# Sinkhorn attention into a gated MLP on one core: the V round trip in halves, another order of the units, the bias off TensorE

## The chip, the cores and the metric

One core of one Trainium2 chip runs the kernel. Its engines are TensorE (PE, with PEld for weight loads), VectorE (DVE), ScalarE (ACT), GpSimd (POOL) and SyncE (SP); each works through its own queue in order, and the two queues of SP and POOL issue all DMAs here. The metric is device time in us. The kernel before took 233.57 us, the median of 3 runs (233.11 to 235.1).

## What is computed

Batch 4, 8 heads, 768 tokens, head size 64, 8 blocks of 96 tokens. A Sinkhorn iteration turns a small matrix per head into mixing weights P; k and v are mixed over blocks with P, q attends within its block, and the result goes through a gated MLP.

```python
for _ in range(5):
    P = P - np.max(P, axis=-1, keepdims=True)
    P = np.exp(P)
    P = P / (np.sum(P, axis=-1, keepdims=True) + 1e-09)
    P = P / (np.sum(P, axis=-2, keepdims=True) + 1e-09)
k_sorted = np.einsum('bhij,bhjcd->bhicd', P, k_b)      # v_sorted likewise
scores = scale * np.matmul(q_b, k_sb.transpose(0, 1, 2, 4, 3))
attn = softmax(scores)                                 # within a block
x = np.matmul(attn, v_sb)                              # -> (B, S, H * D) = (4, 768, 512)
h = np.maximum(x @ w_in, 0.0)                          # d_ff 1024
u, v = h[..., :512], h[..., 512:]
v_n = (v - mu) / np.sqrt(var + 1e-06)
v_s = np.einsum('ts,bsd->btd', w_spatial, v_n) + b_spatial[None, :, None]
out = (u * v_s) @ w_out
```

## The kernel before

Tokens are laid out six to a partition (128 x 6 = 768). Attention of one batch is a list of units. `vmix` (line 234) multiplies v by `pdiag`, a block form of P, for two heads at a time; ACT copies the result into `vm`. After the fourth, the whole `vm` (780 KB) goes to DRAM (`vd`, line 247), and six DMAs bring it back as `vb` (line 250) with the 96 tokens of a block on the partitions. `qtr` and `ktr` bring q and mixed k to head-size-major form; `score` (line 294) and ACT's exponential give `ex`; `attend` (line 316) multiplies `ex` by `vb`, whose 65th column of ones yields the row sums; DVE divides (lines 323, 324). `xtr` transposes the result for the MLP. Each of qtr and xtr serves half of the heads, ktr and vmix two heads, score and attend two heads and half of the blocks.

The MLP of one batch is 13 units: three `vproj` (line 362, with ACT's ReLU and DVE's bn_stats, then the normalisation), four `uproj` (line 393), four `spatial` (line 408, then two matmuls that add the bias, line 414, then DVE's product with u, line 419), three `oproj` (line 430, ACT's copy, a store by SP).

The order on PE, DVE and ACT is that of the code; SP and POOL are placed by the scheduler. First comes attention of batch 0, with the six w_spatial transposes (line 215) in its second half ("the opening"). Then, for each batch, MLP units and units of the next batch's attention alternate, 13 against 28 (three "stages"); the last MLP runs alone ("the tail"). All matmul results go through a PSUM pool of four tiles, so PE waits for whichever engine empties the oldest. All input loads are issued by POOL with a cast to bf16: v and k as one DMA each (rows of 384 elements), q as six (rows of 64).

Of the kernel before, what the change touches and what calls it, by code (L numbers as in the profile page):

```python
# [8 lines left out]
FP32 = mybir.dt.float32  # L9
# [19 lines left out]
def kernel(  # L29
# [12 lines left out]
    nc = tc.nc  # L42
# [25 lines left out]
    moe_pool = ctx.enter_context(tc.tile_pool(name="moe", bufs=5))  # L68
    vsb_pool = ctx.enter_context(tc.tile_pool(name="vsb", bufs=4))
# [13 lines left out]
    b_nat = pers.tile([1, S], FP32)  # L83
    nc.sync.dma_start(out=b_nat, in_=moe_b_spatial.rearrange("(a s) -> a s", a=1))
# [38 lines left out]
    sel16 = const.tile([8, 128], FP32)  # L123
# [9 lines left out]
    e0 = const.tile([128, 128], BF16)  # L133
    nc.vector.memset(e0, 0.0)
    nc.vector.memset(e0[0:1, :], 1.0)
    b_ext = pers.tile([128, S], BF16)
    nc.vector.memset(b_ext, 0.0)
    nc.vector.tensor_copy(
        out=b_ext[0:1, :].rearrange("a (g p) -> a g p", g=G),
        in_=b_nat.rearrange("a (p g) -> a g p", g=G),  # L140
    )
    vm_tiles = []
    for n in range(2):
        vm = pers.tile([128, G, H, VW], BF16, name=f"vm{n}")
# [17 lines left out]

    rowsum = small.tile([BH, NB], FP32, tag="sk")
    colsum = small.tile([BH, NB], FP32, tag="sk2")
    for _ in range(5):
        nc.scalar.activation(out=p_all, in_=p_all, func=AF.Exp)
        nc.vector.reduce_sum(out=rowsum, in_=p_all, axis=AX.X)
        nc.vector.reciprocal(out=rowsum, in_=rowsum)
        nc.vector.tensor_mul(
            out=p_all, in0=p_all, in1=rowsum.to_broadcast([BH, NB, NB]),  # L170
        )
        nc.vector.reduce_sum(
            out=colsum, in_=p_all.rearrange("p i j -> p j i"), axis=AX.X,
        )
# [18 lines left out]
    nc.vector.tensor_copy(out=prep_sb, in_=prep_ps[:, 0, 0:NB * BH])

    pdiag = {}

    def make_pdiag(b, eng, parts=1):
        pd = pd_pool.tile([128, H, NB, TB], BF16, name="pdiag")
        n = H // parts
        for x in range(parts):  # L200
            eng.tensor_mul(
                out=pd[:, x * n:(x + 1) * n],
                in0=_raw_ap(mask16, 0, [mask16.ap[0], [0, n], [TB, NB], [1, TB]]),
                in1=_raw_ap(prep_sb, b * H + x * n, [prep_sb.ap[0], [1, n], [BH, NB], [0, TB]]),
            )
        pdiag[b] = pd.rearrange("p h i t -> p h (i t)")
# [294 lines left out]
```

## Time and profile before

| | |
|---|---|
| median of the runs shown (3) | 233.57 us |
| profiled execution: its time, its span | 233.4 us, 231.4 us |
| granted TensorE clock, mean | 0.884 |
| busy: PE, DVE, ACT, POOL | 73%, 43%, 38%, 17% of the span |
| chain that ended last, by engine | PE 49%, DMA 28%, ACT 8%, DVE 7%, SP's queue 4% |
| opening, three stages, tail (start us) | 0; 60.4, 112.1, 156.3; 200.5 |
| loads queued in the opening | 6 x 768 KB (q, k, v of two batches), w_in 1024, w_spatial 1152, w_out 512 |

The span runs from the first to the last instruction of the profiled execution; its time has 2.0 us more around it. The stages' starts are read off the chain of waits, at the first vproj of each MLP. [...]

### The profile page before, as it was taken

The page shows a single profiled execution, that of the slowest core. Times are in us where ns is not written, and L with a number is a line of the kernel's source. Part 1 is how long each engine was busy: PE and PEld are TensorE (multiplying, and loading weights), DVE is VectorE, ACT ScalarE, POOL GpSimd, SP SyncE. Part 2 cuts the span into 40 slices and gives each one's busy share as a digit, 9 for nine tenths or more (in the row PEclk, how much of TensorE's full clock was granted, in tenths as well). Part 3 has the DMA queues.
Part 4 walks back from the last instruction along what each step waited for, and adds up shares of the span by engine and source line. Part 5 has one row for each costly group of instructions (what it writes and reads, how often), then busy time and mean ns, then how long its engine had stood idle before and what let it go on. Part 6 is the DMA issues. An engine that isn't in the chain of part 4 may idle for free.

```text
span 231.4 us, 3676 instructions
## 1 busy us (share of the span) xinstructions
PE 168.5 (73%) x1551; PEld 105.3 (46%) x1559; DVE 98.8 (43%) x216; ACT 88.3 (38%) x118; POOL 38.8 (17%) x50
## 2 busy tenths in 40 slices
PE   0069000199896707999997599989895999899990
PEld 0037000189654405665465356654553566456530
DVE  5743000076568103555376045553733364475310
ACT  3107400043095701224478522338683124355031
POOL 9945119373016400000000000000000000000000
PEclk9999855555699955999999979999998899999997
DMA  2999999999929997002434600042382001220024
GB/s 25 202 165 223 258 214 195 171 166 205 158 20 224 177 163 109 0 3 91 181 129 79 72 3 0 3 181 91 141 116 25 0 1 69 115 91 3 0 89 185
DMA packets 40306, 25.12 MB, mean 109 GB/s; under 512 B 25825, under 2 KB 37601, under 8 KB 40162
## 3 DMA queue, kind: packets, MB, share of 16 engines
q0 software_dynamic: 34480, 12.19, 46.7%
q1 hardware_dynamic: 5810, 12.70, 20.4%
q8 instruction: 12, 0.20, 0.3%
q14 instruction: 4, 0.03, 0.0%
HBM read 27.59 MB, written 9.49 MB: 160 GB/s over the span
## 4 chain that ended last, share of the span: by engine, by line
PE 49%; DMA 28%; ACT 8%; DVE 7%; SPq 4%; issue 2%; DVEq 0%; ACTq 0%
PE ps L408 15%; DMA vb<-vd 14%; DMA vd<-vm 13%; PE ps L430 9%; PE ps L316 7%; ACT vm L241 5%; PE ps L362 4%; PE ps L294 4%; SPq L250 4%; PE ps L337 3%; PE ps L414 2%; PE ps L393 2%; DVE x_sb L324 2%; PE ps L215 2%; ACT v_sb L370 2%
## 5 line engine op out<-in xcount | busy, mean ns | idle before, releaser
L301 ACT ACTIVATE ex<-ps 96x768 bf16<-96x768 f32 x32 | 25.8, 806 | 74.4 <-PE ps L294 74.4
L316 PE MATMUL ps<-vb,ex 96*96 96x65 bf16 x256 | 19.7, 232 | 35.7 <-DMA vb<-vd 35.7
L408 PE MATMUL ps<-wspT,v_sb 128*128 128x384 bf16 x192 | 38.1, 354 | 0.0
L316 PEld LDWEIGHTS <-ex 96*96 96x96 bf16 x256 | 17.4, 148 | 39.2 <-issue 33.9
L323 DVE RECIPROCAL rec<-ps 96x8 f32<-96x8 f32 x32 | 6.4, 200 | 60.8 <-PE ps L316 60.7
L419 DVE TENSOR_TENSOR gt<-ps,u_sb 128x768 bf16<-128x768 f32 x16 | 15.3, 957 | 26.0 <-PE ps L414 24.4
L408 PEld LDWEIGHTS <-v_sb 128*128 128x128 bf16 x192 | 19.6, 106 | 13.8 <-issue 4.5
L99 POOL DMA_DIRECT2D q_in<-in_q_dram x24 | 21.1, 892 | 16.8 <-DMA wsp_nat<-in_moe_w_spatial_dram 7.3
L373 DVE BATCH_NORM_STATS2 stats<-v_sb 128x6 f32<-128x512 bf16 x24 | 16.3, 677 | 17.4 <-ACT v_sb L370 17.3
L393 PE MATMUL ps<-xt,w_in_sb 128*128 128x384 bf16 x128 | 23.0, 327 | 0.6 <-ACT u_sb L399 0.6
L436 ACT COPY o_sb<-ps 128x1024 f32<-128x1024 f32 x12 | 12.1, 1012 | 29.0 <-PE ps L430 29.0
L362 PE MATMUL ps<-w_in_sb,xt 128*128 128x512 bf16 x95 | 22.6, 382 | 0.6 <-DVE xt L343 0.6
L430 PE MATMUL ps<-w_out_sb,gt 128*128 128x512 bf16 x89 | 22.2, 380 | 0.8 <-DVE gt L419 0.5
L324 DVE TENSOR_TENSOR x_sb<-ps,rec 96x512 bf16<-96x512 f32 x32 | 22.0, 686 | 1.1
L370 ACT ACTIVATE v_sb<-ps 128x1024 bf16<-128x1024 f32 x12 | 12.3, 1023 | 9.1 <-PE ps L362 9.1
L393 PEld LDWEIGHTS <-w_in_sb 128*128 128x128 bf16 x128 | 11.8, 97 | 8.4 <-issue 0.5
L362 PEld LDWEIGHTS <-xt 128*128 128x128 bf16 x96 | 9.3, 99 | 11.3 <-DVE xt L343 1.1
L241 ACT CAST vm<-ps 128x768 bf16<-128x768 f32 x16 | 12.0, 819 | 6.4 <-PE ps L237 6.4
L294 PE MATMUL ps<-qT,kT 64*96 64x96 bf16 x256 | 13.7, 230 | 1.0 <-ACT u_sb L399 0.9
L399 ACT ACTIVATE u_sb<-ps 128x768 bf16<-128x768 f32 x16 | 12.6, 810 | 3.2 <-PE ps L393 3.2
L281 ACT CAST kT<-ps 128x768 bf16<-128x768 f32 x16 | 12.7, 794 | 1.5 <-PE ps L274 1.5
L430 PEld LDWEIGHTS <-gt 128*128 128x128 bf16 x96 | 8.7, 98 | 10.0 <-DVE gt L419 1.0
(62 smaller groups left out, 154.2 us busy)
## 6 DMA issues: line engine op xcount, KB each, us to landing
out_dram<-o_sb SPq DMA_DIRECT2D x12, 512.0 KB, 2.6
vd<-vm SPq DMA_DIRECT2D x4, 780.0 KB, 5.1
vb<-vd SPq DMA_DIRECT2D x24, 130.0 KB, 6.2
v_in<-in_v_dram POOLq DMA_DIRECT2D x4, 768.0 KB, 11.6
k_in<-in_k_dram POOLq DMA_DIRECT2D x4, 768.0 KB, 12.3
q_in<-in_q_dram POOLq DMA_DIRECT2D x24, 128.0 KB, 12.0
wsp_nat<-in_moe_w_spatial_dram POOLq DMA_DIRECT2D x1, 1152.0 KB, 17.9
w_in_sb<-in_moe_w_in_dram POOLq DMA_DIRECT2D x1, 1024.0 KB, 13.8
```

Source lines behind the costliest of these rows:

```text
L99: nc.gpsimd.dma_start(out=t[:, g], in_=_raw_ap(x, b * H * S * D + g * D, [[G * D, 128], [S * D, H], [1, D]]),)
L241: nc.scalar.copy(out=vm[:, :, 2 * hp:2 * hp + 2, 0:D].rearrange("p g h d -> p h g d"), in_=t[:, :, 0:G * D].rearrange("p h (g d) -> p h g ...
L294: nc.tensor.matmul(t[0:BLK, hh, ii * BLK:(ii + 1) * BLK], lhsT=st["k", hp][rows, i * BLK:(i + 1) * BLK], rhs=block_cols(st["q", hp][rows, ...
L301: nc.scalar.activation(out=e.rearrange("p h i c -> p h (i c)"), in_=t[0:BLK, :, 0:NB // 2 * BLK], func=AF.Exp, scale=scale,)
L316: nc.tensor.matmul(t[0:BLK, hh, ii * VW:(ii + 1) * VW], lhsT=e[:, hh, ii, :], rhs=st["vb"][:, i, 2 * hp + hh, :], start=True, stop=True,)
L324: nc.vector.tensor_mul(out=x_sb[:, ih * (NB // 2):(ih + 1) * (NB // 2), hp * 128:hp * 128 + 128] .rearrange("p i (h d) -> p h i d", h=2), ...
L362: nc.tensor.matmul(t[:, x, :], lhsT=xts[b, kc][:, g * 128:(g + 1) * 128], rhs=w_in_sb[:, kc, DH:DFF], start=(kc == 0), stop=(kc == KC - 1),)
L370: nc.scalar.activation(out=v_sb, in_=t, func=AF.Relu)
L373: nc.vector.bn_stats(out=stats, in_=v_sb[:, x, :])
L393: nc.tensor.matmul(t[:, x, 0:HW], lhsT=w_in_sb[:, kc, mc * 128:(mc + 1) * 128], rhs=xts[b, kc][:, x * HW:(x + 1) * HW], start=(kc == 0), s ...
L408: nc.tensor.matmul(t[:, x, 0:HW], lhsT=st["v"][g][:, mc * 128:(mc + 1) * 128], rhs=wspT[:, g, x * HW:(x + 1) * HW], start=(g == 0), stop=F ...
L430: nc.tensor.matmul(t[:, x, :], lhsT=st["gt"][mc][:, g * 128:(g + 1) * 128], rhs=w_out_sb[:, mc, :], start=(mc == 0), stop=(mc == FC - 1),)
```

## The change

The kernel is rewritten around one list of steps per stage; numbers of lines below are those of the changed file where it differs.

- V: `vm` holds the heads in two halves; after vmix 1 and vmix 3 one DMA writes a half (390 KB) and one DMA reads it back, 96 partitions at once, in rows of 260 elements.
- Bias: `b_bc` holds it on all partitions; DVE adds it as it empties PSUM (`vs`, float32), and POOL multiplies by u (DVE does so for the very last). The matmuls with `b_ext` go.
- Loads: q comes in one DMA like v and k. The opening's order is q, v, k of batch 0, w_in, v of batch 1, w_spatial, q and k of batch 1, w_out. Loads of batch b + 2 stand in the stage's list, behind a one-element copy on POOL that reads the second half of `vb`.
- Order: ktr, score and attend come in pairs, the score matmuls alternate between two heads, qtr transposes each head by itself (24 matmuls for 12), all scores of the first two head pairs come before spatial0. The w_spatial transposes move into stage one.
- PSUM copies are split between ACT and DVE: odd vmix and ktr go to DVE, qtr and xtr of the opening to ACT.
- Opening: the P transposes and `sel16` are bf16; filler matmuls (`warm`) stand before and among them; pdiag is made in four pieces.

```diff
+    warm_sb = const.tile([128, 512], BF16)
-        vm = pers.tile([128, G, H, VW], BF16, name=f"vm{n}")
+        vm = pers.tile([128, 2, G, H // 2, VW], BF16, name=f"vm{n}")
...
+    q_in[0] = load_heads(q, 0, "q_in")
+    v_in[0] = load_heads(v, 0, "v_in")
+    k_in[0] = load_heads(k, 0, "k_in")
     w_in_sb = pers.tile([128, KC, DFF], BF16)
     nc.gpsimd.dma_start(out=w_in_sb, in_=moe_w_in.rearrange("(kc p) f -> p kc f", p=128))
+    v_in[1] = load_heads(v, 1, "v_in")
...
+    def warm(n):
+        t = ps_tile()
+        for _ in range(n):
+            nc.tensor.matmul(t[:, 0, :], lhsT=ident_bf, rhs=warm_sb, start=True, stop=True)
...
-        def vmix(hp):
+        def vmix(self, hp, eng):
-            if hp == HP - 1:
-                vd = dram.tile([128, G * H * VW], BF16, name="vd", tag="vd")
-                nc.sync.dma_start(out=vd, in_=vm.rearrange("p g h d -> p (g h d)"))
-                vb = att.tile([BLK, NB, H, VW], BF16, name="vb", tag="vb")
-                for g in range(G):
-                    nc.sync.dma_start(
-                        out=vb[g * TB:(g + 1) * TB].rearrange("t i h d -> t i (h d)"),
-                        in_=vd.rearrange("(i t) (g x) -> g t i x", i=NB, g=G)[g],
-                    )
+            if hp % 2 == 1:
+                vd = dram.tile([128, G * H // 2 * VW], BF16, name="vd", tag=f"vd{half}")
+                nc.sync.dma_start(out=vd, in_=self.vm[:, half].rearrange("p g h d -> p (g h d)"))
+                nc.sync.dma_start(
+                    out=self.vb[:, :, half].rearrange("c i h d -> c i (h d)"),
+                    in_=vd.rearrange("(i t) (g x) -> (t g) i x", i=NB, g=G),
+                )
...
-        def spatial(mc):
+        def spatial(self, mc, eng):
-            for x in range(2):
-                nc.tensor.matmul(
-                    t[:, x, 0:HW], lhsT=e0, rhs=b_ext[:, x * HW:(x + 1) * HW],
-                    start=False, stop=True,
-                )
+            vs = vs_pool.tile([128, 2, HW], FP32, name="vs", tag="vs")
+            nc.vector.tensor_add(
+                out=vs, in0=t[:, :, 0:HW], in1=b_bc.rearrange("p (x c) -> p x c", x=2),
+            )
-            nc.vector.tensor_mul(
-                out=gt.rearrange("p (x c) -> p x c", x=2), in0=t[:, :, 0:HW],
+            eng.tensor_mul(
+                out=gt.rearrange("p (x c) -> p x c", x=2), in0=vs,
...
+        a.qtr(0, ACT), a.qtr(1, ACT)
+        warm(6)
+        spread()
...
+        a.vmix(0, ACT), a.vmix(1, DVE), a.vmix(2, ACT), a.vmix(3, DVE)
+        a.ktr(0, ACT), a.ktr(1, DVE), a.score(0), a.score(1), a.ktr(2, DVE), a.ktr(3, DVE)
+        a.score(2), a.score(3), a.score(4), a.attend(0), a.score(5), a.attend(1)
+        a.attend(2), a.score(6), a.attend(3), a.score(7), a.attend(4), a.attend(5)
+        a.xtr(0, ACT), a.attend(6), a.attend(7), a.xtr(1, ACT)
...
+            steps = """
+                vproj0 vmix0 vproj1 vmix1 vmix2 vproj2 vmix3 qtr0 norm wsp0 uproj0 ktr0 ktr1 wsp1
+                uproj1 qtr1 score0 score1 wsp2 uproj2 ktr2 ktr3 wsp3 load uproj3 score2 score3
+                wsp4 wsp5 spatial0 attend0 attend1 score4 score5 spatial1 attend2
+                attend3 spatial2 score6 score7 attend4 attend5 spatial3 attend6 attend7 xtr0
+                oproj0 oproj1 xtr1 oproj2
+            """.split()
...
+                        nc.gpsimd.tensor_copy(out=gate[:, 0:1], in_=a.vb[0:1, 0, 1, 0, 0:1])
+                        v_in[b + 2] = load_heads(v, b + 2, "v_in")
+                        q_in[b + 2] = load_heads(q, b + 2, "q_in")
+                        k_in[b + 2] = load_heads(k, b + 2, "k_in")
...
+                elif name == "spatial":
+                    m.spatial(n, DVE if last and n == FC - 1 else nc.gpsimd)
```

Three places show how the instructions move. SP's queue, from the opening's first V write to the stores of the first MLP, before and then now (vm_129 and vm_123 are the `vm` of even batches):

```order
L247 DMA vd<-vm_129 128x3120
L250 DMA vb<-vd 16x8x520 x6
L247 DMA vd<-vm_131 128x3120
L250 DMA vb<-vd 16x8x520 x6
L437 DMA out_dram<-o_sb 128x1024 x3
```

```order
L245 DMA vd<-vm_123 128x1560 x2
L246 DMA vb<-vd 96x8x260 x2
L245 DMA vd<-vm_125 128x1560 x2
L246 DMA vb<-vd 96x8x260 x2
L430 DMA out_dram<-o_sb 128x1024 x3
```

Seven issues per V trip are four; both halves' writes stand ahead of the first read-back, though the code has a read-back behind each write.

POOL's queue from the first load on, before (the third batch's loads follow) and now:

```order
L88 DMA v_in<-in_v_dram 128x8x384
L88 DMA k_in<-in_k_dram 128x8x384
L99 DMA q_in<-in_q_dram 128x8x64 x6
L150 DMA w_in_sb<-in_moe_w_in_dram 128x4x1024
L152 DMA wsp_nat<-in_moe_w_spatial_dram 128x4608
L154 DMA w_out_sb<-in_moe_w_out_dram 128x4x512
L88 DMA v_in<-in_v_dram 128x8x384
L88 DMA k_in<-in_k_dram 128x8x384
L99 DMA q_in<-in_q_dram 128x8x64 x6
L201 TENSOR_TENSOR pdiag<-mask_163,prep_sb 128x1024 x3
```

```order
L90 DMA q_in<-in_q_dram 128x8x384
L110 AFFINE_SELECT sel_114<-sel_114 8x128
L90 DMA v_in<-in_v_dram 128x8x384
L90 DMA k_in<-in_k_dram 128x8x384
L130 DMA w_in_sb<-in_moe_w_in_dram 128x4x1024
L90 DMA v_in<-in_v_dram 128x8x384
L133 DMA wsp_nat<-in_moe_w_spatial_dram 128x4608
L90 DMA q_in<-in_q_dram 128x8x384
L90 DMA k_in<-in_k_dram 128x8x384
L137 DMA w_out_sb<-in_moe_w_out_dram 128x4x512
L192 TENSOR_TENSOR pdiag<-mask_147,prep_sb 128x1024 x3
L447 COPY b_bc<-b_nat 128x768
```

q now comes first and in one DMA, v of batch 1 stands ahead of w_spatial, and w_out is last; behind these rows follow the gate copy, three loads and four gate products per stage.

DVE's queue at the front of stage one, from the second v tile's statistics, before and then now:

```order
L373 BN_STATS stats<-v_sb 128x6
L374 BN_AGGR mv<-stats 128x2
L373 BN_STATS stats<-v_sb 128x6
L374 BN_AGGR mv<-stats 128x2
L373 BN_STATS stats<-v_sb 128x6
L374 BN_AGGR mv<-stats 128x2
L373 BN_STATS stats<-v_sb 128x6
L374 BN_AGGR mv<-stats 128x2
L383 TENSOR_SCALAR v_sb<-v_sb,mv,rstd 128x512 x6
L268 COPY qT<-ps 128x1536 x2
```

```order
L366 BN_STATS stats<-v_sb 128x6
L367 BN_AGGR mv<-stats 128x2
L366 BN_STATS stats<-v_sb 128x6
L367 BN_AGGR mv<-stats 128x2
L215 CAST vm_125<-ps 128x2x6x64
L366 BN_STATS stats<-v_sb 128x6
L367 BN_AGGR mv<-stats 128x2
L366 BN_STATS stats<-v_sb 128x6
L367 BN_AGGR mv<-stats 128x2
L215 CAST vm_125<-ps 128x2x6x64
L215 COPY qT<-ps 128x1536
L377 TENSOR_SCALAR v_sb<-v_sb,mv,rstd 128x512 x6
```

Copies of vmix results (vm_125) and of k now stand between the statistics and behind the normalisation (TENSOR_SCALAR); qT is copied once ahead of the normalisation.

## Rows read from the trace of the kernel before

**Rows 1.** The page, section 1: busy us, share of the span, instructions.

```profile
PE 168.5 (73%) x1551; PEld 105.3 (46%) x1559; DVE 98.8 (43%) x216; ACT 88.3 (38%) x118; POOL 38.8 (17%) x50
```

**Rows 2.** Waits, longest first: who waited for whom, us, times, longest.

```profile
PE ps L316 <- DMA vb<-vd: 35.7, 4, 21.7
```

**Rows 3.** The chain that ended last, opening: start us, us, what.

```profile
19.74 12.30 DMA vd<-vm
...
34.33 10.83 DMA vb<-vd
45.24 0.82 PE ps L316 x8
...
59.39 1.29 PE ps L337 x16
```

**Rows 4.** The same chain, the three stages.

```profile
68.07 8.48 DMA vd<-vm
...
90.05 3.08 PE ps L408 x12
93.13 0.33 PE ps L414 x2
...
94.25 1.95 PE ps L408 x12
...
118.89 5.15 DMA vd<-vm
...
126.37 5.80 DMA vb<-vd
...
177.95 3.50 PE ps L408 x12
```

**Rows 5.** Stretches: length, busy by engine, PEclk, DMA share, GB/s.

```profile
20.00:25.00 5.00, 3.51 (x76) 2.83 (x76) 1.92 (x2) 3.80 (x6) 1.10 (x2) 1.00 1.17 251
...
55.00:60.40 5.40, 5.40 (x66) 5.25 (x65) 4.93 (x10) 0.81 (x1) 0.00 (x0) 0.50 1.68 187
...
sum 51.70, PE 39.77 PEld 24.22 DVE 22.94 ACT 20.43 POOL 7.05; mean PE 6.63 PEld 4.04 DVE 3.82 ACT 3.41 POOL 1.18
...
156.30:200.50 44.20, 39.23 (x376) 23.68 (x376) 21.16 (x42) 21.34 (x28) 0.00 (x0) 0.96 0.27 73
```

**Rows 6.** The page, section 6: DMA issues, count, KB each, us to landing.

```profile
vd<-vm SPq DMA_DIRECT2D x4, 780.0 KB, 5.1
...
v_in<-in_v_dram POOLq DMA_DIRECT2D x4, 768.0 KB, 11.6
...
wsp_nat<-in_moe_w_spatial_dram POOLq DMA_DIRECT2D x1, 1152.0 KB, 17.9
w_in_sb<-in_moe_w_in_dram POOLq DMA_DIRECT2D x1, 1024.0 KB, 13.8
```

**Rows 7.** POOL's timeline from 0, and v_in's landings by tile.

```profile
2.49 1.04 POOL L88 DMA_DIRECT2D v_in<-in_v_dram  x1
...
13.98 0.55 POOL L152 DMA_DIRECT2D wsp_nat<-in_moe_w_spatial_dram  x1 [2.93 <-DMA k_in<-in_k_dram]
...
DMA to landing us min/median/max: 7.4/11.6/26.7
```

**Rows 8.** PE's timeline in stage two: start us, us, line, shapes, count.

```profile
118.60 0.83 PE L262 MATMUL ps<-ident_bf,q_in 128*128 128x128 bf16 x12
119.36 0.53 PE L274 MATMUL ps<-pdiag,k_in 128*64 128x128 bf16 x12
```

**Rows 9.** Groups by line and shape: count, busy us, mean ns, idle before.

```profile
L373 DVE BATCH_NORM_STATS2 stats<-v_sb 128x6 f32<-128x512 bf16 x24 | 16.3, 677 | 17.4 <-ACT v_sb L370 17.3
L419 DVE TENSOR_TENSOR gt<-ps,u_sb 128x768 bf16<-128x768 f32 x16 | 15.3, 957 | 26.0 <-PE ps L414 24.4 <-PE ps L294 1.6
...
L241 ACT CAST vm<-ps 128x768 bf16<-128x768 f32 x16 | 12.0, 819 | 6.4 <-PE ps L237 6.4
...
L201 POOL TENSOR_TENSOR pdiag<-mask,prep_sb 128x1024 bf16<-128x1024 bf16 x3 | 5.9, 2007 | 0.0
```

More of the change, by code (lines that the diff above doesn't have):

```diff
@@ L193 @@
[L193 to L206, printed above, removed]
@@ L435, in oproj @@
             o_sb = o_pool.tile([128, 2, DM], FP32, name="o_sb", tag="o")
-            nc.scalar.copy(out=o_sb, in_=t)
+            copy(eng, o_sb, t)
             nc.sync.dma_start(
-                out=out[b].rearrange("(p g) n -> p g n", g=G)[:, 2 * n:2 * n + 2, :], in_=o_sb,
-            )
-        order = (
-            [(vproj, n) for n in range(3)] + [(uproj, n) for n in range(FC)]
-            + [(spatial, n) for n in range(FC)] + [(oproj, n) for n in range(3)]
-        )
-        return [lambda f=f, a=a: f(a) for f, a in order]
@@ new lines, in oproj @@
+                in_=o_sb,
+            )
+    ACT, DVE = nc.scalar, nc.vector
+    with tc.manual_schedule(engines={ET.PE, ET.DVE, ET.Activation, ET.Pool}):
+        a = Attention(0)
+        sinkhorn()
+        warm(4)
+        a.qtr(0, ACT), a.qtr(1, ACT)
+        warm(6)
+        spread()
+        for h in range(0, H, 2):
+            make_pdiag(0, DVE, h, 2)
+        for b in range(1, B):
+            make_pdiag(b, nc.gpsimd, 0, H)
+        nc.gpsimd.tensor_copy(
+            out=b_bc.rearrange("p (g c) -> p g c", g=G),
+            in_=b_nat.rearrange("p (c g) -> p g c", g=G),
+        )
+        a.vmix(0, ACT), a.vmix(1, DVE), a.vmix(2, ACT), a.vmix(3, DVE)
[3 more added lines that the diff above has]
+        a.xtr(0, ACT), a.attend(6), a.attend(7), a.xtr(1, ACT)
+        for b in range(B):
+            m = Gmlp(b)
+            last = b == B - 1
+            a = None if last else Attention(b + 1)
+            steps = """
[5 more added lines that the diff above has]
+            """.split()
+            for step in steps:
+                name, n = step.rstrip("0123456789"), int(step[-1]) if step[-1].isdigit() else None
+                if name == "wsp":
+                    if b == 0:
+                        wsp_unit(n)
+                elif name == "load":
+                    if b + 2 < B:
+                        gate = small.tile([1, 2], BF16, name="gate", tag="gate")
+                        nc.gpsimd.tensor_copy(out=gate[:, 0:1], in_=a.vb[0:1, 0, 1, 0, 0:1])
+                        v_in[b + 2] = load_heads(v, b + 2, "v_in")
+                        q_in[b + 2] = load_heads(q, b + 2, "q_in")
+                        k_in[b + 2] = load_heads(k, b + 2, "k_in")
+                elif name in ("vproj", "uproj"):
+                    getattr(m, name)(n)
+                elif name == "spatial":
+                    m.spatial(n, DVE if last and n == FC - 1 else nc.gpsimd)
+                elif name == "norm":
+                    m.norm()
+                elif name == "oproj":
+                    m.oproj(n, ACT)
+                elif not last:
+                    if name in ("vmix", "ktr"):
+                        getattr(a, name)(n, ACT if n % 2 == 0 else DVE)
+                    elif name in ("qtr", "xtr"):
+                        getattr(a, name)(n, DVE)
+                    else:
+                        getattr(a, name)(n)
```

307 lines of the change are left out of this document (142 added, 165 removed).

## The prediction

> **What bounds the kernel now.** The page's first section [rows 1] shows TensorE (PE) busy 168.5 of 231.4 us, so some 63 us of the span are PE standing still. The list of waits names the largest block: PE's attend matmuls (line 316) waited 35.7 us, in four pieces, for the read-back of V, `vb`, the longest piece 21.7 us [rows 2]. The chain of waits gives the places. In the opening attention the write to DRAM (`vd`) starts at 19.74 and takes 12.30 us, the last read-back lands at 45.2 (34.33 + 10.83), and only then do the attends run, 8 matmuls in 0.82 us [rows 3]. In stage one (MLP of batch 0 beside attention of batch 1) `vd` takes 8.48 us; in stage two, where no load is under way, 5.15, and the last read-back 5.80 [rows 4]. After each such stall PE is slow: twelve spatial matmuls take 3.08 or 3.50 us, later ones 1.95 [rows 4]. [...] The stretches are also the budgets: stage one lasts 51.7 us with PE busy 39.77, stage three 44.2 with 39.23. So a stage is PE's work plus one wait for V, and the opening is DMA.
>
> **The sum is made against the profiled execution,** 233.4 us with a span of 231.4. The median shown is 233.57, 0.2 above it; I take the two as one.
>
> **Opening (0 to 60.4).** Bytes first. The opening queues q, k and v of two batches, w_in, w_spatial and w_out: 6 x 768 + 1024 + 1152 + 512 = 7296 KB; with the V trip, 2 x 780, it is 8856 KB, 9.07 MB [rows 6], with w_out's 512 KB from the table above. q now comes in rows of 384 elements, as v and k do, no longer 64. For such rows there is a rate: v, issued at 2.49, landed 7.4 us later, at 9.9, and k behind it in the queue had landed when w_spatial's issue stopped waiting at 13.98 [rows 7]. That is 768 KB in 4 us, 200 GB/s. With larger rows and `vd` beside them 251 GB/s moved between 20 and 25 us [rows 5]. In the new order q lands first, at about 9.5, v at 13.4, k at 17.
>
> So vmix starts no earlier. PE's queue now holds 48 q transposes and 6 warm-up matmuls ahead of the transposes of P. They begin at 9.5; 12 of k's form take 0.53 at full clock [rows 8], so twice that at the slow one: 48 end near 13.5, and 6 x 512 columns near 15.5. The chain behind them is shorter than before (8 bf16 transposes for 16 passes, one 256-column matmul, two copies, pdiag for two heads), and vmix comes at about 17.5. vmix0's copy is on ACT, vmix1's on DVE behind four pieces of pdiag; the first half's `vd` leaves at about 19.7, where the whole one left before. b_ext's copy leaves the Sinkhorn loop, which q's landing covers.
>
> From there DMA decides. Beside the loads, `vd` got 780 KB in 12.3 us, 63 GB/s [rows 3, 6]. At that share both halves are written by 32, the first by 27. SP's new order (above) has both writes ahead of the first read-back, so reading goes on from about 28: 780 KB more, in rows of 520 B for 1040. At 63 to 76 GB/s the second half lands at 43 to 46. The other way round, 9.07 MB, 3.1 of them at 200 GB/s until 21 and the rest at 250, leave all queues empty at about 45. I take 44. Lower bound: the quiet durations, 5.15 and 8.1 (124.04 to 132.17 [rows 4]) from 19.7, give 33. Upper: all bytes at 200 GB/s from 6 on, 51. Scores 0 to 4 and attends 0 to 3 run while PE waits for the second half. Behind it stand four attends of 0.8, two xtr of 1.3 [rows 3] and one round of DVE between them, 1.2: 44 + 7 = 51 against 60.4. **Term -9.4**, bounds -20 and -2. The w_spatial transposes, which ran here, are paid below.
>
> [...] The row shows 63 of about 250, a quarter, and the sum goes by the row.
>
> **Stage one.** PE's 39.77 is the base. Out go the bias matmuls, 4 x 0.33, and the slow pass, 3.08 - 1.95 and about 0.9 on attends and scores beside it [rows 4]. In come the w_spatial transposes, 6 x 6 at full clock, half of 0.83 for six [rows 8], 2.5; qtr, 24 narrow transposes for 12 wide ones, 1.06 for 0.83, twice, 0.5; and a wait of 1.1 of the first vproj, since the opening's last xt copy is on ACT. The wait for V goes: in stage two attend0 came 20 us behind the stage's start (112.1 to 132.2), the new order puts spatial0 and two more scores ahead of it, and a half trip of 390 KB needs some 8 to 10 us after its vmix (half of 5.15 and of 8.1, and a fixed part). Half two is wanted four attends later.
>
> What is late next is DVE. It now empties vmix1, vmix3 and two k tiles, 0.82 each, and in its queue vmix1's copy stands behind two pairs of bn_stats, 4 x 0.68 and their aggregates [rows 9]. PSUM has four tiles, so PE stops at qtr0 for about 1 us and again, behind the normalisation, at uproj1 and score1. I take 2.0 a stage; bounds 0 (ACT and DVE keep up, as they did for 10 us on end in the spatial rounds) and 6 (each of six such tiles 1 us late). Sum: 39.8 - 1.3 - 2.0 + 2.5 + 0.5 + 1.1 + 2.0 = 42.6 against 51.7. **Term -9.1.**
>
> **Stages two and three.** 39.2 - 1.3 - 1.55 (3.50 - 1.95) + 0.5 + 2.0 = 38.9 against 44.2. **Term -10.6** for the two.
>
> What I cost at nothing, and its cover. *The gate on POOL:* the nearest row is pdiag there, 2007 ns for 1024 elements [rows 9], 1.5 for 768. Four of these lie beside spatial rounds of 3 us, and the last one beside two attends, xtr0 and six matmuls of oproj0, 3.1 us, against 0.96 + 1.5 and the hops. *The bias add* on DVE is a pass like the old gate, 0.957 [rows 9], in its old place; DVE's busy time of a stage goes from 21.2 [rows 5] by four copies to 24.5 of 39. *The new wait:* a one-element copy on POOL waits for the second half of V; queued behind it are three load issues of about 1 us and the four gates. V lands some 20 us into a stage, so the first gate comes at 24, and oproj0 wants the fourth at 33. The loads themselves have 20 us until vmix of the next stage, and three at 4 us need 16. SP's stores of the last MLP stand ahead of the next `vd`, but end before vmix does. *Score and ktr in pairs:* no row shows a gap at such a switch, so 0, and up to 1 us of gain a stage in the range.
>
> **Tail.** Three bias passes go, 1.0. At the fourth, add and gate follow each other on DVE, 1.9 us, beside which oproj does six matmuls where it did three: 0. **Term -1.0.**
>
> 233.4 - 9.4 - 9.1 - 10.6 - 1.0 = 203.3. **I predict 203 us.**
>
> **Rivals.**
> A. *The V trip gets half of the DMA engines.* 1560 KB at 125 GB/s from 21.7 land at 36 instead of 44: 195. For it: beside `vd` lay loads with the largest rows (w_in, w_spatial), now mostly shorter ones. Against: read-back rows of 520 B.
> B. *DVE sets the pace of each stage's front.* Six late tiles at 1 us, 4 more than I take, three times: 215. For it: bn_stats, copies and normalisation stand in one queue and in that order. Against: DVE's sum has room.
> C. *Slower than before, by the gate on POOL.* In a stage about 12 us are there for four products, 3 each; in the tail 1.8 each. Beyond that a gate of P us costs 4 x (P - 3) in each of three stages and 3 x (P - 1.8) in the tail. It eats the 30 us from P = 4.7 on; at 5 the time is 237. The row gives 1.5, and 3 if float32 input cost double, which is short of it.
> D. *The halves don't pipeline.* With SP's order both could land together at 44; attends 0 to 3 and three scores, 5 us at the slow clock, move behind it: 208.
>
> Chances: forecast 0.47, A 0.2, B 0.17, D 0.13, C 0.03. The range, 192 to 216, holds the forecast's bounds and the middles of A, B and D; half of B and the far end of A are out, with C. A difference under 1% can't be told from none here. Faster by over 1% 0.95, within 1% 0.02, slower 0.03: only C, or several costs together, gets there.
>
> **What would show it.** Right: no wait of PE for `vb` after the opening, a granted clock near 1 from stage one on, stages of 43, 39 and 39, V's second half landed at 44 and the first vproj at 51, a gate of 1.5 us. Wrong: `vb` at 36 (A), PE waiting for DVE's copies in a stage's front (B) or oproj for POOL (C), attend0 and attend4 let go together (D). It falls most easily on V's landing in the opening, since both my ways to it use rates of other row sizes.

## Result, and the profile after

The changed kernel took **215.33 us** (median of 4 runs, 212.83 to 216.15), the kernel before 233.34 beside it (4 runs, 231.97 to 235.1): a ratio of 0.919, 95% interval 0.908 to 0.930. That lies inside the range of 192 to 216 and 12 us above the 203 of the forecast. The profiled execution took 216.15 us, with a span of 214.4. It is the longest of the four, at a granted clock of 0.884 where the others had 0.890 to 0.905, and the ratio is taken without it.

The first section of the page after; columns as in [rows 1], which it answers to. PE has shed hardly any work (168.5 before); DVE has gained 29.8 us, where the forecast counted four copies of 0.82 a stage, some 10 us in all.

```profile
PE 167.0 (78%) x1621; PEld 102.0 (48%) x1630; DVE 128.6 (60%) x229; ACT 94.1 (44%) x105; POOL 47.7 (22%) x46
```

The list of waits, which answers to [rows 2]: 35.7 us in four waits became 10.0 in two, both in the opening, for the first half at 41.85 and for the second at 47.22. No stage waits for V any more, as forecast.

```profile
PE ps L313 <- DMA vb<-vd: 10.0, 2, 9.2
```

On PE's timeline the two are these:

```profile
41.85 0.85 PE L313 MATMUL ps<-vb,ex 96*96 96x65 bf16 x8 [9.16 <-DMA vb<-vd]
...
47.22 1.49 PE L313 MATMUL ps<-vb,ex 96*96 96x65 bf16 x16 [0.87 <-DMA vb<-vd]
```

The chain that ended last, opening and the middle of stage two (start us, us, what), for [rows 3, 4].

```profile
16.33 6.87 DVE pdiag L192 x4
...
23.25 0.84 PE ps L231 x2
...
25.14 9.56 DMA vd<-vm
...
34.72 12.45 DMA vb<-vd
...
47.22 1.49 PE ps L313 x16
...
54.50 2.74 PE ps L355 x6
...
113.56 2.63 DVE kT L215
...
116.23 2.25 PE ps L387 x8
...
119.94 2.74 DVE kT L215
```

The chain runs through the second of the two V writes. The first leaves at 24.16, on SP's timeline:

```profile
24.16 1.32 SPq L245 DMA_DIRECT2D vd<-vm  x2
```

Two things stand here that the sum didn't have: 6.87 us of `pdiag` in DVE's queue ahead of its copy of vmix1, so that the V trip leaves at 24.2 and not at 19.7, and copies of k that take 2.7 us each. The groups by line and shape (count, busy us, mean ns, idle before), which answer to [rows 9], give their price:

```profile
L215 DVE CAST kT<-ps 128x768 bf16<-128x768 f32 x9 | 24.3, 2726 | 9.4 <-PE ps L270 9.4
L213 ACT CAST kT<-ps 128x768 bf16<-128x768 f32 x7 | 19.1, 2728 | 2.3 <-PE ps L270 2.3
L215 DVE CAST vm<-ps 128x768 bf16<-128x768 f32 x8 | 7.5, 940 | 0.0
L192 DVE TENSOR_TENSOR pdiag<-mask,prep_sb 128x256 bf16<-128x256 bf16 x4 | 6.9, 1774 | 0.0
L192 POOL TENSOR_TENSOR pdiag<-mask,prep_sb 128x1024 bf16<-128x1024 bf16 x3 | 6.5, 2200 | 5.7 <-DVE prep_sb L186 5.7
L412 POOL TENSOR_TENSOR gt<-vs,u_sb 128x768 bf16<-128x768 f32 x15 | 24.6, 1640 | 79.0 <-DVE rec L321 57.0 <-DVE vs L408 19.0 <-ACT ex L298 3.1
```

The same 768 float32 to bf16 out of PSUM cost 0.94 us on DVE as `vm` and 2.73 as `kT`, on ACT no less; and a quarter of a pdiag took DVE 1.77 us, nearly as long as POOL takes for a whole one. POOL's gate at 1.64 us is what was counted (1.5).

The three stages as stretches (length, busy by engine, granted clock, DMA share, GB/s), for [rows 5]:

```profile
52.77:100.70 47.93, 41.76 (x430) 25.42 (x430) 30.50 (x52) 22.65 (x24) 9.45 (x8) 0.90 0.49 97
100.70:142.64 41.94, 37.58 (x392) 23.12 (x392) 27.53 (x46) 21.86 (x24) 9.43 (x8) 0.96 0.61 133
142.64:185.06 42.42, 37.35 (x392) 22.73 (x392) 27.53 (x46) 21.82 (x24) 6.56 (x4) 0.96 0.23 76
```

### The profile page after: what moved, and what is told of

Read it like the earlier page. It is cut to its first block, busy times and chain, and to the rows that moved or that the text cites. A ratio compares the mean times of both kernels' runs of the same rounds, so it can differ in the third digit from the quotient of the medians.

```text
span 214.4 us, 3826 instructions
## 1 busy us (share of the span) xinstructions
PE 167.0 (78%) x1621; PEld 102.0 (48%) x1630; DVE 128.6 (60%) x229; ACT 94.1 (44%) x105; POOL 47.7 (22%) x46
## 4 chain that ended last, share of the span: by engine, by line
PE 49%; DVE 22%; DMA 14%; ACT 9%; POOL 3%; issue 2%; DVEq 0%; ACTq 0%; SPq 0%; POOLq 0%
PE ps L402 13%; PE ps L355 9%; PE ps L423 8%; PE ps L387 7%; DMA vb<-vd 6%; DMA vd<-vm 4%; DVE vs L408 4%; DVE kT L215 4%; ACT kT L213 4%; DMA q_in<-in_q_dram 4%; DVE pdiag L192 3%; DVE vm L215 3%; PE ps L313 3%; POOL gt L412 2%; DVE stats L366 2%; PE ps L335 2%
## 5 line engine op out<-in xcount | busy, mean ns | idle before, releaser
L412 POOL TENSOR_TENSOR gt<-vs,u_sb 128x768 bf16<-128x768 f32 x15 | 24.6, 1640 | 79.0 <-DVE rec L321 57.0
L298 ACT ACTIVATE ex<-ps 96x768 bf16<-96x768 f32 x32 | 24.3, 804 | 33.5 <-PE ps L291 22.3
L402 PE MATMUL ps<-wspT,v_sb 128*128 128x384 bf16 x192 | 33.3, 326 | 1.7 <-ACT ex L298 1.4
L387 PE MATMUL ps<-xt,w_in_sb 128*128 128x384 bf16 x128 | 26.4, 359 | 4.9 <-DVE kT L215 2.7
L215 DVE CAST kT<-ps 128x768 bf16<-128x768 f32 x9 | 24.3, 2726 | 9.4 <-PE ps L270 9.4
L408 DVE TENSOR_TENSOR vs<-ps,b_bc 128x768 f32<-128x768 f32 x16 | 15.3, 958 | 18.2 <-PE ps L402 18.0
L313 PE MATMUL ps<-vb,ex 96*96 96x65 bf16 x256 | 17.1, 225 | 10.5 <-DMA vb<-vd 10.0
L355 PE MATMUL ps<-w_in_sb,xt 128*128 128x512 bf16 x92 | 24.2, 405 | 1.3 <-ACT xt L213 1.1
L213 ACT CAST kT<-ps 128x768 bf16<-128x768 f32 x7 | 19.1, 2728 | 2.3 <-PE ps L270 2.3
L291 PE MATMUL ps<-qT,kT 64*96 64x96 bf16 x256 | 12.1, 228 | 7.3 <-ACT kT L213 5.0
```

What stands on the lines that cost most here:

```text
L213: nc.scalar.copy(out=out, in_=in_)
L215: nc.vector.tensor_copy(out=out, in_=in_)
L298: nc.scalar.activation(out=e.rearrange("p h i c -> p h (i c)"), in_=t[0:BLK, :, 0:NB // 2 * BLK], func=AF.Exp, scale=scale,)
L313: nc.tensor.matmul(t[0:BLK, hh, ii * VW:(ii + 1) * VW], lhsT=self.e[n][:, hh, ii, :], rhs=self.vb[:, i, h // (H // 2), h % (H // 2), :], s ...
L355: nc.tensor.matmul(t[:, x, :], lhsT=self.xt[kc][:, g * 128:(g + 1) * 128], rhs=w_in_sb[:, kc, DH:DFF], start=(kc == 0), stop=(kc == KC - 1),)
L387: nc.tensor.matmul(t[:, x, 0:HW], lhsT=w_in_sb[:, kc, mc * 128:(mc + 1) * 128], rhs=self.xt[kc][:, x * HW:(x + 1) * HW], start=(kc == 0), ...
```

## The experiments

All times are in us. The stages' starts are read off PE's timeline in each trace, at the first vproj of each MLP; the ratio is to the kernel before, on the same chip (medians of 233.4 to 233.8, 7 runs each time). The e runs, the f runs and the g runs had a chip each. The rows without a label are from the sections above.

| kernel | median | ratio, 95% | first vproj | stages one, two, three | tail |
|---|---|---|---|---|---|
| before | 233.3 | 1 | 60.4 | 51.7, 44.2, 44.2 | 30.9 |
| forecast | 203 | | 51 | 42.6, 38.9, 38.9 | 29.9 |
| after | 215.3 | 0.908 to 0.930 | 52.8 | 47.9, 41.9, 42.4 | 29.3 |
| e1_kt_write_rows | 205.7 | 0.872 to 0.884 | 53.1 | 45.2, 37.8, 38.1 | 29.3 |
| e2_pdiag_late | 211.0 | 0.893 to 0.906 | 49.2 | 47.9, 42.0, 40.8 | 29.2 |
| e3_both | 199.4 | 0.846 to 0.859 | 48.2 | 43.9, 37.8, 37.8 | 29.3 |
| e4_loads_behind_v | 192.6 | 0.817 to 0.827 | 41.5 | 43.7, 37.8, 37.8 | 29.3 |
| f1_whole_trip | 200.5 | 0.852 to 0.862 | 49.9 | 44.0, 37.8, 37.8 | 29.3 |
| f2_bias_on_pe | 202.4 | 0.860 to 0.873 | 48.7 | 44.5, 38.7, 38.7 | 29.5 |
| f3_loads_free | 201.8 | 0.856 to 0.868 | 49.4 | 43.9, 38.5, 37.8 | 29.3 |
| f4_scores_by_head | 200.7 | 0.853 to 0.861 | 49.1 | 44.8, 37.9, 37.9 | 29.3 |
| g1_old_order | 207.6 | 0.881 to 0.897 | 49.3 | 48.1, 40.0, 40.0 | 29.3 |
| g2_six_reads | 207.2 | 0.881 to 0.894 | 50.0 | 44.3, 43.9, 37.8 | 29.5 |
| g3_warm_wait | 190.6 | 0.812 to 0.822 | 39.5 | 44.1, 37.8, 37.8 | 29.3 |
| g4_q_rows64 | 202.6 | 0.858 to 0.874 | 50.6 | 45.0, 38.9, 37.8 | 29.4 |

e4, f1 to f4, g1 and g4 start from e3, g2 from f1, g3 from e4. In e3 and the runs that start from it with q's load as it was, the first vmix comes between 15.7 and 17.6, as that load lands; so a difference of a microsecond in the first vproj is not read as an effect.

**The two mis-priced steps.** e1 writes k's copy in the order of its own memory:

```diff
-                kT.rearrange("p (it g) -> p g it", g=G),
-                t[:, 0:S].rearrange("p (g it) -> p g it", g=G),
+                kT.rearrange("p (it g) -> p it g", g=G),
+                t[:, 0:S].rearrange("p (g it) -> p it g", g=G),
```

> Theory: the copy of the mixed k into kT takes 2.73 us (0.80 before) because its innermost loop writes 2-byte elements 12 bytes apart; with the same destination written in its own order, and the stride on the PSUM side, it takes 0.8 to 1.0 us, the stages come from 42 to about 39 us, and the whole from 215 to about 204 us (two such copies per stage, about 3.7 us, lie on the chain, and the opening has one pair on its path under the wait for V). Rival: a stride costs the same on either side; copies stay at 2.7 and the time at 215.

Its groups of the k copies:

```profile
L215 DVE CAST kT<-ps 128x768 bf16<-128x768 f32 x9 | 8.5, 953 | 6.1 <-PE ps L270 6.1
L213 ACT CAST kT<-ps 128x768 bf16<-128x768 f32 x7 | 5.6, 794 | 2.3 <-PE ps L270 2.3
```

The stride now lies on the side of PSUM (128 float32, 512 B), and 953 and 794 ns are about what a copy that reads in order takes (`vm` in the same run, 940 on DVE and 806 on ACT). Stages two and three fall by 4.2 and 4.3 us, stage one by 2.7. The change writes 2-byte elements 12 bytes apart (2726 ns on DVE, 2728 on ACT); the kernel before wrote runs of 16 elements, on ACT (794 ns). What makes the first form slow no run shows; no other spacing of single elements was timed.

e2 moves POOL's share of `pdiag` (batches 1 to 3) and the bias copy behind the four vmix, held there by a one-element copy of what vmix1's copy wrote into `vm`:

```diff
+        a.vmix(0, ACT), a.vmix(1, DVE), a.vmix(2, ACT), a.vmix(3, DVE)
+        hold = small.tile([1, 2], BF16, name="hold", tag="gate")
+        nc.gpsimd.tensor_copy(out=hold[:, 0:1], in_=a.vm[0:1, 0, 0, 2, 0:1])
         for b in range(1, B):
             make_pdiag(b, nc.gpsimd, 0, H)
...
-        a.vmix(0, ACT), a.vmix(1, DVE), a.vmix(2, ACT), a.vmix(3, DVE)
```

> Theory: DVE's four pdiag pieces take 1.77 us each (0.37 by their length) because POOL's pdiag of the later batches runs at the same time and each piece waits for one of POOL's to end. Held until vmix1's copy is done, the pieces take about 0.4, the first V write leaves at 19.5 instead of 24.2. If the share of the DMA engines decides, V's second half then lands 3 to 5 us earlier and the time is about 211. Rival: the landing is set by when all queued loads are through (about 47 us); then the write leaves earlier, V lands at 46 to 47 all the same, and the time stays at 214 to 215.

DVE's, POOL's and SP's timeline of e2 (start us, us):

```profile
16.53 1.43 DVE L192 TENSOR_TENSOR pdiag<-mask,prep_sb 128x256 bf16<-128x256 bf16 x4
```

```profile
19.06 5.94 POOL L192 TENSOR_TENSOR pdiag<-mask,prep_sb 128x1024 bf16<-128x1024 bf16 x3
```

```profile
18.94 1.18 SPq L245 DMA_DIRECT2D vd<-vm  x2
```

Apart, four pieces take DVE 1.43 us; together with POOL they took 6.87. In the change the vmix pairs, each let go by one piece, came 2.15 us apart (from 16.81 to 23.25 us), where one POOL product took 2.20. So from the second on a piece of DVE's took about as long as a whole product of POOL's beside it; why, the traces do not say. V's trip leaves at 18.9 for 24.2, and its second half lands at 43.6 for 47.2: of 5.2 us only 3.5 arrive. The loads still move beside it; e4 below tests what they cost.

e3 is both edits.

> Both edits. Additive by the theories: about 200 with V landing earlier, 204 if the landing stays where the loads set it.

A stretch of e3, stage two, shows what is left:

```profile
92.10:129.88 37.78, 35.67 (x393) 22.13 (x392) 24.08 (x46) 18.43 (x24) 9.47 (x8) 1.00 0.68 148
```

PE is busy 35.67 of 37.78 us at a clock of 1.00: the stage is PE's work. At 199.4 us the kernel without the two slips is 4 us under the forecast.

**Which part carries the gain.** e4 holds the loads that are not wanted soon (q and k of batch 1, w_spatial, w_out) until the first half of V is back.

```diff
+        hold2 = small.tile([1, 2], BF16, name="hold", tag="gate")
+        nc.gpsimd.tensor_copy(out=hold2[:, 0:1], in_=a.vb[0:1, 0, 0, 0, 0:1])
+        q_in[1] = load_heads(q, 1, "q_in")
+        nc.gpsimd.dma_start(out=wsp_nat, in_=moe_w_spatial.rearrange("(p g) s -> p g s", g=G))
+        k_in[1] = load_heads(k, 1, "k_in")
...
```

> Both edits, and the opening's loads of q and k of batch 1, w_spatial and w_out wait on POOL for the first half of V to be back. Theory that queued bytes set V's landing in the opening: with 3.4 of 9.4 MB taken out of its way V's second half lands at 30 to 35 instead of 47 and stage one starts 10 us or more earlier; part of it is lost if w_spatial or k arrive late in stage one: 190 to 196. Rival: V's trip is slow for its own row sizes whatever is queued; then V lands at 44 or later and the late loads only cost: 204 or more.

The first attend starts at 31.57 for 38.02 although the first vmix came 1.7 us later, and the first vproj comes 6.7 us earlier, less than the 10 expected: in the opening V waits for bytes that nobody needs yet (6.5 us at the first attend).

f1 sends V as one write and one read-back per batch:

```diff
-            if hp % 2 == 1:
...
+            if hp == HP - 1:
...
+                nc.sync.dma_start(out=vd, in_=self.vm.rearrange("p g h d -> p (g h d)"))
                 nc.sync.dma_start(
-                    out=self.vb[:, :, half].rearrange("c i h d -> c i (h d)"),
+                    out=self.vb.rearrange("c i h d -> c i (h d)"),
                     in_=vd.rearrange("(i t) (g x) -> (t g) i x", i=NB, g=G),
                 )
```

> From the kernel with both mends (199.4 us), V goes again as one whole vm (780 KB) after the fourth vmix: one write, one read-back in rows of 520 elements; the order of the units is untouched. Theory, halves matter in the opening only: the write leaves some 4 us later (after vmix3 instead of vmix1), nothing can be attended until all has landed, so attends 0 to 3 and three scores (some 4 us at the slow clock) move behind it; in the stages V still comes before attend0, whose place in the list is far enough behind: 203 us (201.5 to 206), stages still 37.8. Rival, the order of the units did nothing without the halves: stages two and three wait for vb again, some 3 us each, 210 us or more. Second rival, the opening's bytes alone decide: 199 to 200.

The second rival came nearest (200.5 for its 199 to 200). From the first vmix to the first attend of the opening it is 22.8 us (17.11 to 39.91) against 22.3 with halves (15.72 to 38.02), and the stages are the same. SP's timeline and POOL's, stage two:

```profile
103.98 0.33 SPq L244 DMA_DIRECT2D vd<-vm  x1
107.29 0.33 SPq L245 DMA_DIRECT2D vb<-vd  x1
```

```profile
113.14 0.18 POOL L476 COPY gate<-vb 1x1 bf16<-1x1 bf16 x1 [23.91 <-DMA vb<-vd]
```

The whole trip takes 9.1 us in a quiet stage, and attend0 comes at 113.67, 0.5 us after it: in time, if barely.

g2 puts the six read-backs of the kernel before in place of f1's one.

```diff
-                nc.sync.dma_start(
-                    out=self.vb.rearrange("c i h d -> c i (h d)"),
-                    in_=vd.rearrange("(i t) (g x) -> (t g) i x", i=NB, g=G),
-                )
+                for g in range(G):
+                    nc.sync.dma_start(
+                        out=self.vb.rearrange("(t g) i h d -> g t i (h d)", g=G)[g],
+                        in_=vd.rearrange("(i t) (g x) -> g t i x", i=NB, g=G)[g],
+                    )
```

> From the kernel with V as one whole trip (200.5 us), the read-back is six DMAs of 16 rows of partitions, as in the kernel before; the new order of units stays. Theory, the form of the read-back counts: alone, six took 8.1 us from the first issue where one takes 5.7, and with 0.6 us to spare in a stage the attends wait some 2 to 4 us in each of three stages, 207 to 212 us. Rival, only the order of the units counts: 200 to 201.

The time came out as expected, its mechanism did not: stage three does not wait for V, and 6.1 us sit in stage two. POOL's timeline and PE's there:

```profile
111.00 0.18 POOL L477 COPY gate<-vb 1x1 bf16<-1x1 bf16 x1 [21.34 <-DMA vb<-vd]
111.49 0.94 POOL L90 DMA_DIRECT2D v_in<-in_v_dram  x1 [0.32 <-issue]
```

```profile
118.45 1.46 PE L313 MATMUL ps<-vb,ex 96*96 96x65 bf16 x16 [4.19 <-issue]
...
120.65 3.83 PE L402 MATMUL ps<-wspT,v_sb 128*128 128x384 bf16 x12
```

The gating copy reads one partition, and so waits for the first of six read-backs only. The loads of batch 3 start at 111.5, and PE stands 4.2 us and is slow behind it (3.83 for 2.12 us). The profile names no releaser for this stop; but of the six read-backs, issued from 107.7 to 111.9, one took 6.4 us to land, where in stage three none took over 3.1. Stage three has no loads; there the six take at most 9.7 us for the trip and V is still in time. By these two stages it is the loads, let go too early, that cost the 6 us. The number of read-backs is not what made the trip of the kernel before long, 13.3 us (118.9 to 132.2 [rows 4]). Of that, the write alone took 5.15 us where f1's and g2's, of the same form and size, take 3.3; and g2's reads go to every sixth partition, since k's token order has changed, those of before to 16 adjacent ones. Which of these shortened it was not tried.

f3 leaves the gate of those loads out.

```diff
-                        gate = small.tile([1, 2], BF16, name="gate", tag="gate")
-                        nc.gpsimd.tensor_copy(out=gate[:, 0:1], in_=a.vb[0:1, 0, 1, 0, 0:1])
```

> From the kernel with both mends (199.4 us), the one-element copy that holds the loads of batch b + 2 back is left out; they stand at the same place of POOL's queue. Theory: batch 2's loads then start in the opening as soon as their buffers come free (v after vmix3, q after qtr1, k after ktr3, about 21 us), 2304 KB beside the V trip: at the rates of the opening V's second half lands 4 to 9 us later, 204 to 208 us; stage two's loads start behind the last gate of stage one and are over before the next V write, nothing there. Rival, queued loads share one queue in order and batch 2's come behind what is queued already, so V's landing is unchanged: 199 to 200.

The forecast for the opening was wrong, its rival right: batch 2's loads are issued at 26 to 29, but first vmix to first attend stays 22.45 us (16.69 to 39.14). That they stand behind what is queued already is the rival's reason; the trace shows no more than that V's time did not change. Stage two is 0.7 us longer, where nothing was expected. The two intervals overlap, so of the whole difference, 2.4 us, little is sure.

g1 gives the stages the old order of units (14 of the MLP, not the 13 told above):

```diff
...
+                vproj0 vmix0 vmix1 vproj1 vmix2 vmix3 vproj2 norm qtr0 ktr0 wsp0 uproj0 qtr1
+                ktr1 wsp1 uproj1 score0 ktr2 wsp2 uproj2 score1 ktr3 wsp3 uproj3 attend0 score2
+                attend1 wsp4 wsp5 load spatial0 score3 attend2 spatial1 score4 attend3 spatial2
+                score5 attend4 spatial3 score6 xtr0 oproj0 attend5 score7 oproj1 attend6
+                attend7 xtr1 oproj2
```

> From the kernel with both mends (199.4 us), the units of a stage stand in the order of the kernel before (its alternation of 14 MLP units with 28 attention units, single scores, attend0 right behind uproj3); V still goes in halves with one read-back each, and the w_spatial transposes stay in stage one. Theory, the shorter trip alone takes the wait for V away: the halves land 14 and 19 us into a stage and attend0 and attend4 are due at about 18 and 26, so at most 1 us of waiting, and single scores cost 0.2 us more each pair: 203 us, stages 39 to 39.5. Rival, the order did it: PE waits 3 us or more for vb in each stage and runs slow behind it, 209 us or more.

No stage waits for V here either, so the new trip alone, in halves with one read-back each, does away with that wait. Yet the stages are 4.2, 2.2 and 2.2 us longer than e3's, more than the theory had without a wait. Stage two of g1:

```profile
97.37:137.38 40.01, 36.67 (x393) 22.26 (x392) 24.51 (x46) 18.59 (x24) 9.43 (x8) 1.00 0.65 140
```

PE is busy 1.0 us more, half of it in the scores (3.0 for 2.5), and idle 1.2 more, in small waits for copies (x, k, u and the MLP's v). In stage one the granted clock was lower as well, 0.89 for 0.94. The new order is worth 8 us of e3's 34, by that and not by V.

f2 takes the bias back to PE; one DVE pass multiplies out of PSUM, and POOL has no gates.

```diff
-            vs = vs_pool.tile([128, 2, HW], FP32, name="vs", tag="vs")
-            nc.vector.tensor_add(
-                out=vs, in0=t[:, :, 0:HW], in1=b_bc.rearrange("p (x c) -> p x c", x=2),
-            )
+            for x in range(2):
+                nc.tensor.matmul(
+                    t[:, x, 0:HW], lhsT=e0, rhs=b_ext[:, x * HW:(x + 1) * HW],
+                    start=False, stop=True,
+                )
...
-            eng.tensor_mul(
-                out=gt.rearrange("p (x c) -> p x c", x=2), in0=vs,
+            nc.vector.tensor_mul(
+                out=gt.rearrange("p (x c) -> p x c", x=2), in0=t[:, :, 0:HW],
```

> From the kernel with both mends (199.4 us), the bias is added by two matmuls per spatial again and DVE multiplies by u straight out of PSUM; POOL has no gates. Theory, PE sets the pace of a stage: 32 matmuls of 384 columns at 0.16 to 0.17 us come back, 5.3 us, less up to 1 in the tail, where one DVE pass replaces add and POOL product: 204 us (203 to 205), stages 39.1. Rival, the stages wait for DVE and POOL as much as for PE: within 1 us of 199.4, or faster.

Its matmuls of the bias, and its stage two:

```profile
L412 PE MATMUL ps<-b_ext,e 128*128 128x384 bf16 x32 | 7.8, 326 | 0.0
```

```profile
93.17:131.90 38.73, 36.63 (x400) 22.94 (x400) 24.12 (x46) 18.43 (x24) 2.81 (x4) 1.00 0.67 144
```

PE's busy time grows by 0.96 us and the stage by 0.95: what leaves PE comes off the stage one for one. At 202.4 us the kernel is under the 203 to 205 expected, since a stage paid 0.95 where 1.3 was counted. The tail is 0.2 longer than e3's, so there the change gains 0.2, not 1.0.

f4 runs a head's four score matmuls before the other's, where they alternated.

```diff
-            for ii in range(NB // 2):
-                i = ih * (NB // 2) + ii
-                for hh in range(2):
+            for hh in range(2):
+                for ii in range(NB // 2):
+                    i = ih * (NB // 2) + ii
```

> From the kernel with both mends (199.4 us), the four score matmuls of one head come before the four of the other, as in the kernel before; they alternated. Theory: matmuls of two heads use different halves of the rows and overlap when they alternate; a pair of scores takes 0.56 us now where one score alone took 0.39 before, so 4 pairs a batch cost 0.2 each more, 3.5 us in all: 203 us, and a pair's row of about 0.78. Rival, the overlap comes from the pairing of the steps alone: 199.4 and a row of 0.56.

The rival held for the scores: a pair that follows another step takes 0.60 to 0.62 us in stage two, 0.56 to 0.62 in e3, and stages two and three are within 0.1 us. The other 1.3 us of the time are ahead of that: the first vproj comes 0.9 later, which is not read as an effect, and stage one is 0.9 longer, its second vproj slow (2.82 us for 2.00). Running scores in pairs saves time (g1: 2.5 us of scores a stage for 3.0); the order within a pair does not show, nor, then, that the matmuls of two heads overlap because they alternate.

g4 loads q again in rows of 64 (of 256 B in DRAM).

```diff
...
+        for g in range(G):
+            nc.gpsimd.dma_start(
+                out=t[:, g],
+                in_=_raw_ap(x, b * H * S * D + g * D, [[G * D, 128], [S * D, H], [1, D]]),
+            )
```

> From the kernel with both mends (199.4 us), q is loaded again as six DMAs of rows of 64 elements per batch; all else as there. Theory, rows of 128 B fp32 words cost the opening in two ways: six issues (5 us on POOL) put v's load later by 4 us, and q of two batches moves at some 160 to 185 GB/s for 205, 2 us; vmix and V come 3 to 7 us later, nothing in the stages: 203 to 207. Rival, the queue holds enough work that the form of q's rows is hidden: 199 to 200.5.

202.6 is just under the theory's 203 to 207, and its interval touches e3's. In the profiled execution, the longest of the four with 204.1, k lands late (ktr waits 1.5 us for it) and the first vproj comes at 50.6, 2.4 later than e3's. But the stages pay as well, where nothing was expected: in stage two the six q issues stand on POOL ahead of the gates (such six took 1.06 and 4.42 us in the opening), PE waits 1.28 us for DVE's bias add, where in e3 it waits 0.2 at most, and the stage is 1.1 longer. So q's one DMA is worth at most 3.2 us, and at most 2.4 of them in the opening.

**A version that beats both.** g3 is e4 with fillers while PE waits for V.

```diff
-        a.score(2), a.score(3), a.score(4), a.attend(0), a.score(5), a.attend(1)
+        a.score(2), a.score(3), a.score(4)
+        warm(34)
+        a.attend(0), a.score(5), a.attend(1)
```

> From the kernel with V ahead of the later loads (192.6 us), 34 filler matmuls of 512 columns stand before the opening's attend0, 7.2 us at full clock in a wait of 8.7. Theory: the granted clock falls to 0.5 because PE stands idle in that wait, so with the fillers the attends, xtr and first vproj behind it run at 1.0 and the first vproj comes 3 to 4 us earlier: 189 us (188 to 190.5). Rival, the copies on DVE and ACT set the pace of that stretch, or the clock falls all the same: 192 to 193. On the other side: the fillers outlast the wait, 193.5 to 197.

At 190.6 us it is 2.0 faster than e4 (190.2 to 190.6 for 191.9 to 193.1), less than expected. The two ran on different chips and the intervals of their ratios overlap; what the traces show is a first vproj 2.05 us earlier. Its stretches from the fillers on:

```profile
20.00:31.00 11.00, 9.29 (x89) 4.76 (x85) 2.10 (x3) 2.90 (x4) 6.19 (x4) 1.00 1.17 244
31.00:38.00 7.00, 6.62 (x104) 6.19 (x105) 5.50 (x14) 4.43 (x5) 3.27 (x5) 0.76 0.93 137
38.00:45.00 7.00, 6.08 (x28) 2.84 (x28) 1.09 (x3) 2.63 (x4) 0.00 (x0) 0.51 1.07 206
```

The first attends take 0.51 to 0.55 us for eight matmuls (0.85 in e4, at a granted clock of 0.50). Then, some 3.5 us behind the wait, PE slows: sixteen attend matmuls take 1.16 us from 34.27 and 1.46 from 36.51, where eight took 0.51 at 32.50 and at 33.28; the granted clock is 0.76 over 31 to 38 and 0.51 over 38 to 45. PE was busy 9.29 of the 11 us up to 31, with 1.25 idle at their end while V was not yet back, and 2.94 of the 3.3 behind. The gain ends there, and the theory's reason, an idle PE, is not shown to be the whole one.

## Why the forecast was right, and where it was not

The forecast's frame held: no wait for V in a stage, gate and bias add hidden, each stage PE's work and a small rest. The 12 us are two prices; without them (e3) the time is 199, so the two cost 16 us and the other terms were 4 too high. That 215.3 lies within the range is in part luck: the misses cancel in part, and the upper end was set to hold rival B's 215 and D's 208, neither of which came about as described.

- **"It now empties vmix1, vmix3 and two k tiles, 0.82 each": failed.** They cost 2.73, on both engines. I took the price of a `vm` copy for every copy of 768 elements, though the diff changes the order in which k is written. e1 gives 10 us back. Rival B's 215 was met at its place, the front of a stage with PE waiting for copies, but not by its cause: with the same queue order and short copies PE's waits for copies of k, from both engines, fall from some 11 us to 1.2 (e3). PE's waits for DVE's vm copies, which B had, are 2.4 in both.
- **"and vmix comes at about 17.5", the first write at about 19.7: failed by POOL.** The first vmix came at 16.8, the second pair 2.15 later and so on; DVE could copy vmix1 only behind all four pieces, and `vd` left 4.5 us late (24.2 for 19.7). e2 and e3 give 4 to 6 us back. The sum left 2.2 us for DVE's four pieces and the copy (17.5 to 19.7), as if DVE worked alone; I did not ask what POOL does beside it.
- **"I take 44" for V's landing: held, given its start.** With `vd` at 18.9 (e2) V's second half landed at 43.6; in the change, with `vd` at 24.2, at 47.2. DMA decides there, as said. In the change V's 1560 KB took 23.0 us, 69 GB/s of 222 in all, so the half of rival A, an estimate from the 251 GB/s of [rows 5], was not granted; only moving the loads away helped (e4). (Rival A's own sum was off: 1560 KB at 125 GB/s from 21.7 end at 34.5, not 36.) Behind the second half the sum had 7 us to the first vproj; they were 5.5.
- **Stage one, 42.6: mis-sized.** Even without the two slips it takes 43.9 (e3). The w_spatial transposes cost 3.0 where I had 2.5, and the first vproj run slow, 2.74 us for six where eight take 1.89 later (in e4, where the six take as long, the granted clock is 0.50 over 41.5 to 45.4), which I had ended with the opening. The clock was not near 1 from stage one on: 0.90, 0.96 and 0.96 in the change, 0.94, 1.00 and 1.00 in e3.
- **Stages two and three, 38.9: right but for k.** e3 has 37.8; for the "I take 2.0 a stage" of DVE's lateness stand 2.1 us of idle PE of all causes, and PE's work is 1.2 less than counted. Score and ktr in pairs, "up to 1 us of gain a stage", was too careful: the whole order is worth 2.2 us in such a stage (g1), 0.5 of it in the scores' own time.
- **The bias, 1.3 a stage: 0.95** (f2). **The tail, 1.0:** the tail is 1.6 shorter, of which the bias is 0.2 (f2). Some 0.7 lie behind the last copy of the output (3.7 us to the end of the span for 4.4); where the rest comes from was not tried.
- **Rival C** fell as reasoned: 1.64 us a gate. **Rival D** did not happen: attend0 was let go at 41.85 and attend4 at 47.22, 5.4 us apart. Yet the halves bought no time, since with V as a whole the first attend starts nearly as early (f1).

So the words of the change mislead about its parts. The halves of V's trip are worth nothing that these runs can tell; six read-backs or one make at most 0.6 us of a quiet trip (9.7 and 9.1). The wait for V went with a trip 4 us shorter, for which no single cause is shown; the order of the units is worth 8 us by other waits, the bias 3. Open as well is what the shorter P chain and the new order of the opening's loads gave to the opening, for which no run stands.

## What to carry to other kernels

Here a copy's price went by how its output lay in memory, at the same element count (on DVE 2.73 us, or 0.95 in e1): when a diff changes a rearrange, price it anew, and if one side must be strided, try the PSUM side. Before two engines are given pieces of one job, time them side by side (four pieces of DVE's took 6.87 us beside POOL's, 1.43 apart). Once a stage is PE's work alone (e3, 35.67 of 37.78 us), only PE's instructions and small waits count; a transfer that is merely in time is worth as much as an early one (f1's stage two, with V 0.5 us ahead of its use, takes 37.8 as well).

## What the runs showed of the hardware that was not expected

- 768 elements of bf16 written 12 bytes apart took 2.73 us on DVE and on ACT, against 0.95 and 0.79 in order; the latter read PSUM 512 bytes apart and was about as fast as a copy that reads in order (0.94 and 0.81, `vm`).
- Four pdiag pieces took DVE 1.43 us alone and 6.87 beside POOL's; POOL's own went from 2.00 to 2.20 us each.
- After 11 us at a granted clock of 1.00 with PE busy for 9.29 of them, a pause of 1.25 at their end included, the clock was 0.76 over the next 7 us, with PE busy for 6.62, and 0.51 over the 7 behind (g3). What that hangs on was not settled.
